# One core, attention with memory beside a gated feed-forward: the first loads regrouped, one more dummy matmul, and the last output tiles interleaved and halved

## The chip, the core and the metric

The kernel runs on one NeuronCore of a Trainium2 chip. Five engines work side by side and meet at semaphores: PE (TensorE: matmuls, with its weight loads listed as PEld), ACT (ScalarE), DVE (VectorE), POOL (GpSimd) and SP (SyncE), which here only issues transfers. ACT can issue transfers too. Transfers issued by SP go through one queue, those issued by ACT through another; both are served by the same 16 DMA engines.

The metric is the time of one execution on the device in microseconds. Before the change the median of five runs is 278.86 us (277.49 to 280.86). The profiled execution took 277.49 us, and its profile covers a span of 275.8 us.

## The reference

The input `A_x` has 2048 tokens of 512 numbers in bf16. Two branches read it, and a gate per token mixes them:

```
g = sigmoid((x * gate_w).sum(-1))
a = attention(x) @ wo          # 32 heads of 16, four segments of 512 tokens
b = (relu(x @ W_gate) * (x @ W_up)) @ W_down      # 512 -> 1792 -> 512
out = g * a + (1 - g) * b
```

In each segment of 512 tokens the attention is causal softmax attention within the segment, mixed (by `sigmoid(beta)` per head) with a read of a linear memory M, z, to which earlier segments have added their keys and values. `B_x` is not used.

## The kernel before

**A planner writes the order.** `program` describes every step as an `Op` with an estimated duration, the tiles that it reads and writes, and the engines that can do it. `Sched` then simulates the engines with these estimates and, for each engine, places the next ready operation of the queue with the lowest priority number (`_choose`, L285; the queues are filled in L798 to L821). What comes out is a fixed list of instructions and semaphore waits for each engine. On the chip only that order and those waits remain, not the estimated times. A queue is taken from its head only. Attention has priority 0 on PE, memory steps 1, projections 2, output tiles 3 (`pout`, L802) and the feed-forward 4 (`pffn`, L803), so the feed-forward fills what the others leave free.

**The start** (L410 to L506). The first 512 tokens are loaded as four tiles of 128 tokens into slots `hT0` to `hT3`, alternately by SP and ACT, 128 KB each. Then SP loads the two column halves of `wq` and ACT those of `wk`, 256 KB each in rows of 512 bytes; then each loads one half of `wv`. SP goes on with `braw` (the 32 values of beta, spread to all partitions), the first halves of the feed-forward weights (`wg0`, `wu0`, 896 KB each), `gwc` (the gate weights as one column, elements of 2 bytes), four transposing loads that bring segment 1 as `xT1` (L434), and later `wg1`, `wu1`, `wo`, `wd`. PE has meanwhile done five dummy matmuls (`warm(5, 0, 3)`, L492), and transposes the four token tiles by multiplying with an identity (`fx`, L494); DVE and ACT copy the results from PSUM to `xT` (L503, L505). One more dummy matmul, `warm(1, 1, 0)` (L506), stands between these transposes and the first projection.

**Projections and attention.** For segment s, `proj(s)` (L559) multiplies in the order q0, k0, q1, k1, q2, k2, q3, k3, v0 to v3; each waits for its weights by name (`wq0` for its column half, and so on). One "quad" (L665) computes scores for four heads at a time into the four PSUM banks `psL`, ACT exponentiates the whole (L670), POOL masks the diagonal blocks (L673), and L690 multiplies with the values. As `psL` is one buffer, the next quad waits for the exponential before it. L590 and L581 are exponentials of keys and queries for the memory; L511 is the exponential of beta.

**The feed-forward and the output.** `ffn(c)` (L725) makes, for each of 14 blocks f, a gate product and an up product (L735, four matmuls each) into two of the four PSUM banks `psA`; ACT or DVE takes the relu (L743, L744) and DVE multiplies the two into a tile of `hT` (L746). `outp(s)` (L749) makes four output tiles of 128 tokens. Each is 18 matmuls into one bank: four with `oT` and `wo` (L758, `oa`), 14 with `hT` and `wd` (L766, `ob`, placed two at a time). Then ACT or DVE scales the bank into one of two buffers `osb` (L771, L770), and SP stores it (L773). In the last segment, s = 3, the first matmuls of a tile ask for only ten of the 14 `hT` tiles, so a tile can begin before the feed-forward is finished.

A rule in `Sched.ready` (L209 to L216) keeps an output tile from starting on PE long before its reader could run: it may start no earlier than the end of what the reader must also wait for (here the store that frees its `osb` buffer), less its own length and 300 ns. At most two output tiles hold banks at once (`CAPS`, L87).

Of the kernel before, what the change touches and what calls it, by code (L numbers as in the profile page):

```python
# [84 lines left out]
class Sched:  # L85
# [114 lines left out]
    def ready(self, op, e):  # L200
        t0 = self.now[e]
        t = op.after
        for p in self._pred_done(op, e):
            if not p.done:
                return None
            if self.know[e][p.stream] < p.idx:
                t = max(t, p.end + LAT)
        if op.ep is not None:
            if op.role == "w" and op.ep.bank is None:  # L209
                for rd in op.ep.readers:  # L210
                    for p, _ in rd.preds:
                        if p.ep is op.ep or p.cidx > op.cidx:
                            continue
                        if not p.done:
                            return None
                        t = max(t, p.end - op.occs["pe"] - 300.0)  # L216
                bc = self._bank_choice(op, e)
                if bc is None:
                    return None
                t = max(t, bc[1])  # L220
            elif op.ep.bank is None:
                return None
        if e == "pe" and t > 0:
            t += 80.0
        return max(t, t0)
# [115 lines left out]
def plan(S, D, F):  # L341
    NT, KT, NF = S // 128, D // 128, F // 128
    return [
        ("xT", [128, KT, S], BF16), ("wq", [128, KT, 512], BF16), ("wk", [128, KT, 512], BF16), ("wv", [128, KT, 512], BF16),
        ("wo", [128, 4, 512], BF16), ("wg", [128, KT, F], BF16), ("wu", [128, KT, F], BF16), ("wd", [128, NF, 512], BF16),
        ("qT", [128, 8, 512], BF16), ("kT", [128, 4, 512], BF16), ("kp", [128, 12, 512], BF16),
        ("phiq", [128, 4, 512], BF16), ("ek", [128, 4, 512], BF16), ("phik", [128, 4, 512], BF16), ("ttmp", [128, 2, 512], BF16),
        ("vaug", [128, 2, 4, 32, 17], BF16), ("E", [128, 8, 4, 512], BF16),
        ("Tn", [128, 2, 512], F32), ("adT", [128, 512], BF16), ("oTt", [128, 512], BF16),
        ("amem", [128, 2, 512], BF16), ("amemT", [128, 4, 512], BF16), ("oT", [128, 8, 512], BF16),  # L350
        ("hT", [128, 20, 512], BF16), ("rl", [128, 3, 512], BF16), ("osb", [128, 2, 512], BF16),
        ("Mbd", [128, 4, 136], F32), ("Mbd16", [128, 4, 136], BF16), ("mumask", [128, 2, 136], BF16), ("mutmp", [128, 2, 136], F32),
        ("gwc", [128, KT], BF16), ("braw", [128, 32], BF16), ("eb", [128, 32], F32), ("romgh", [128, 32], F32), ("epsv", [128, 32], F32),
        ("gexp", [128, NT], F32), ("omg", [128, NT], F32), ("gexpT", [128, NT * 4], F32), ("c2g", [128, NT, 32], F32),
        ("rden", [128, 32], F32), ("rdg", [128, 32], F32), ("rdm", [128, 128], F32), ("pm8", [128, 8], F32), ("pm", [128, 2], F32), ("ident", [128, 128], BF16),
    ]
# [23 lines left out]
def program(sc, nc, T, PL, PA, A_x, A_wq, A_wk, A_wv, A_wo, A_beta, W_g, W_u, W_d, gate_w, out, NSEG, KT, NF, NT, EPS, SCALE):  # L380
# [20 lines left out]
    def dma(eng, fn, nbytes, occ=500.0, **k):  # L401
        return op(eng, fn, occ, dma=True, nbytes=nbytes, **k)
# [9 lines left out]
    def load(eng, names, dst, src, nbytes, occ=460.0):  # L412
        (lact if eng == "act" else lsp).append(dma(eng, lambda e, dst=dst, src=src: e.dma_start(dst, src), nbytes, occ=occ, writes=names, name="ld" + names[0]))  # L413
    x0 = A_x[0, 0:512, :].rearrange("(i p) d -> p i d", p=128)
    for i, eng in enumerate(("sp", "act", "sp", "act")):
        load(eng, [f"hT{i}"], V.hT[:, i, :], x0[:, i, :], 1 << 17)
    for h in range(2):
        for nm, w, src, eng in (("wq", V.wq, A_wq, "sp"), ("wk", V.wk, A_wk, "act")):
            load(eng, [f"{nm}{h}"], w[:, :, 256 * h:256 * h + 256], src.rearrange("(kt p) n -> p kt n", p=128)[:, :, 256 * h:256 * h + 256], 1 << 18)
    for h, eng in enumerate(("sp", "act")):  # L420
        load(eng, [f"wv{h}"], V.wv[:, 2 * h:2 * h + 2, :], A_wv.rearrange("(kt p) n -> p kt n", p=128)[:, 2 * h:2 * h + 2, :], 1 << 18)
    wgr = W_g.rearrange("(kt p) n -> p kt n", p=128)
    wur = W_u.rearrange("(kt p) n -> p kt n", p=128)
    half = (NF // 2) * 128
# [7 lines left out]
    def load_x(c):  # L432
        for kt in range(KT):
            lsp.append(dma("sp", lambda e, c=c, kt=kt: e.dma_start_transpose(V.xT[:, kt, c * 512:(c + 1) * 512], A_x[0, c * 512:(c + 1) * 512, kt * 128:(kt + 1) * 128]),  # L434
                           1 << 17, occ=1280.0, writes=[f"xT{c}_{kt}"], name=f"ldx{c}_{kt}"))
    load("sp", ["braw"], V.braw[:], A_beta.partition_broadcast(128), 8192)
    load_gu(0)
    gsrc = gate_w.rearrange("(kt p) -> p kt", p=128)

    def ld_gw(e):  # L440
        with nc.allow_non_contiguous_dma(reason="one column of gate weights"):
            return e.dma_start(V.gwc[:], gsrc)
    lsp.append(dma("sp", ld_gw, 60000, writes=["gwc"], name="ldgw"))
    load_x(1)
    load_gu(1)
    load("sp", ["wo"], V.wo[:], A_wo.rearrange("(g p) n -> p g n", p=128), 1 << 19)
# [38 lines left out]
    def warm(n, k, b):  # L485
        def fn(e):
            for i in range(n):
                ins = e.matmul(PL[:, b, :], lhsT=V.rl[:, 0, 0:128], rhs=V.rl[:, 0, :], start=True, stop=True)
            return ins
        return pe(fn, n * 427, reads=["rl0"], writes=[f"bankL{b}"], name=f"warm{k}")  # L490

    xps, xcs = [warm(5, 0, 3)], []  # L492
    for i in range(4):
# [5 lines left out]
        for h in range(2):  # L499
# [3 lines left out]
                xcs.append(dve(lambda e, d=dst, s_=srcp: e.tensor_copy(d, s_), t_dve(256), reads=[f"bankL{i}"], writes=[f"xT0_{i}a"], name=f"xc{i}"))  # L503
            else:
                xcs.append(act(lambda e, d=dst, s_=srcp: e.activation(d, s_, ACT.Copy), t_act(256), reads=[f"bankL{i}"], writes=[f"xT0_{i}b"], name=f"xc{i}"))  # L505
    xps.append(warm(1, 1, 0))  # L506
    sc.queue(0, xps)
    sc.queue(0, [t for t in xcs if t.eng == "dve"])
    sc.queue(0, [t for t in xcs if t.eng == "act"])
# [49 lines left out]
    def proj(s):  # L559
# [3 lines left out]
        def pj(w, col, name, wname, tokmajor=False):  # L563
            ep = Epoch("proj")

            for k0 in range(0, KT, 2):
                def fn(e, k0=k0):
                    for kt in (k0, k0 + 1):
                        if tokmajor:
                            ins = e.matmul(A(ep)[:, :], lhsT=V.xT[:, kt, tok + col * 128:tok + (col + 1) * 128], rhs=w[:, kt, :], start=(kt == 0), stop=(kt == KT - 1))  # L570
                        else:
                            ins = e.matmul(A(ep)[:, :], lhsT=w[:, kt, col * 128:(col + 1) * 128], rhs=V.xT[:, kt, tok:tok + 512], start=(kt == 0), stop=(kt == KT - 1))  # L572
                    return ins
                pes.append(pe(fn, mm(512, 2), reads=[f"{wname}{k0 // 2 if tokmajor else col // 2}"] + xt(s), name=f"{name}{s}_{col}", ep=ep, role="w2" if k0 else "w"))
            return ep
        for G in range(4):
            ep = pj(V.wq, G, "q", "wq")
# [169 lines left out]
        return pes, evs, slots  # L747

    def outp(s, slots):  # L749
        pes, evs, sps = [], [], []  # L750
        for i in range(4):
            t = 4 * s + i
            ep = Epoch("out")
            o0 = (s % 2) * 4

            def fa(e, i=i, ep=ep):
                for G in range(4):
                    ins = e.matmul(A(ep)[:, :], lhsT=V.oT[:, o0 + G, i * 128:(i + 1) * 128], rhs=V.wo[:, G, :], start=(G == 0), stop=False)  # L758
                return ins
            pes.append(pe(fa, mm(512, 4), reads=[f"oT{o0 + G}" for G in range(4)] + ["wo", "wd"] + [f"hT{x}" for x in (slots if s < NSEG - 1 else slots[:NF - 4])], name=f"oa{s}_{i}", ep=ep, role="w"))  # L760
            for f0 in range(0, NF, 2):
                fs = list(range(f0, min(f0 + 2, NF)))

                def fb(e, i=i, ep=ep, fs=fs):
                    for f in fs:
                        ins = e.matmul(A(ep)[:, :], lhsT=V.hT[:, slots[f], i * 128:(i + 1) * 128], rhs=V.wd[:, f, :], start=False, stop=(f == NF - 1))  # L766
                    return ins
                pes.append(pe(fb, mm(512, len(fs)), reads=[f"hT{slots[f]}" for f in fs] + ["wd"], name=f"ob{s}_{i}_{f0}", ep=ep, role="w2"))
            r = t % 2
            evs.append(sc.add(Op([("dve", lambda e, ep=ep, r=r, t=t: e.tensor_scalar(V.osb[:, r, :], A(ep)[:, :], V.omg[:, t:t + 1], None, ALU.mult), t_dve(512)),  # L770
                                  ("act", lambda e, ep=ep, r=r, t=t: e.activation(V.osb[:, r, :], A(ep)[:, :], ACT.Copy, scale=V.omg[:, t:t + 1]), t_act(512, True, 1))],  # L771
                                 reads=[f"omg{min(s, 1)}"], writes=[f"osb{r}"], name=f"fin{s}_{i}", ep=ep, role="r")))
            sps.append(dma("sp", lambda e, r=r, t=t: e.dma_start(out[0, t * 128:(t + 1) * 128, :], V.osb[:, r, :]), 1 << 17, reads=[f"osb{r}"], writes=[f"out{t}"], name=f"st{t}"))  # L773
        return pes, evs, sps

    Q = {k: [] for k in ("patt", "pnd", "pmu", "pproj", "pffn", "pout", "exp", "aphi", "dproj", "dsb", "datt", "dnd", "dmu", "effn", "eout", "pool", "poolmu", "spk", "spa", "spo")}

# [21 lines left out]
    sc.queue(1, Q["pmu"])  # L799
    sc.queue(1, Q["pnd"])  # L800
    sc.queue(2, Q["pproj"])
    sc.queue(3, Q["pout"])  # L802
    sc.queue(4, Q["pffn"])  # L803
    sc.queue(0, Q["exp"])
    for px in ("q", "k"):
        sc.queue(2, [t for t in Q["aphi"] if t.name.startswith(px)])
# [55 lines left out]
```

## Time and profile before

| quantity | value |
|---|---|
| median of five runs | 278.86 us |
| profiled execution, its own time | 277.49 us |
| its span | 275.8 us |
| PE busy | 268.5 us, 97% |
| DVE busy | 197.1 us, 71% |
| ACT busy | 191.9 us, 70% |
| first projection matmul starts | 6.51 us |
| last matmul group ends | 272.57 us |
| HBM read and written | 8.14 MB, 2.10 MB |

Times are microseconds from the start of the span. A PE row such as "260.75 1.03 ... x4" is a group of four matmuls that starts at 260.75; its length includes the time that the last one needs to run through the array. So four matmuls of 512 columns show as 1.03, but the next group starts 0.86 to 0.87 later: the step from one to the next is 0.216. Brackets at the end of a row give the idle time of the engine just before it and what ended that. SPq and ACTq are transfers being issued. "From issue to landing" is the time from the start of the issuing instruction to the semaphore that says that all data are there.

### The profile page before, as it was taken

The numbers are of one execution on the slowest core, as the hardware profiler recorded it, in microseconds if no ns is written. First come the engines' busy times: TensorE is split into PE (matmuls) and PEld (weight loads), VectorE is DVE, ScalarE is ACT, GpSimd is POOL, SyncE is SP. The second block draws the span as 40 slices with busy tenths as digits, with TensorE's granted clock in tenths as the row PEclk, the third lists the DMA queues.
The fourth block names the chain that finished last, engine by engine and source line by source line (L and its number), as shares of the span: only waits on it lengthen the run. The fifth ranks groups of instructions, "written<-read, shape, count | busy, mean of one in ns | idle before, by whom it ended". The sixth has DMA issues, their size and how long they took to land.

```text
span 275.8 us, 5326 instructions
## 1 busy us (share of the span) xinstructions
PE 268.5 (97%) x2182; PEld 114.8 (42%) x2182; DVE 197.1 (71%) x389; ACT 191.9 (70%) x171; POOL 94.0 (34%) x152
## 2 busy tenths in 40 slices
PE   7999999999999999999999999999999999999895
PEld 3344444544444444444344443444434344444342
DVE  5788998999979999977979781768764336872300
ACT  4499898788578878776698776767778777822301
POOL 4032342535344724452433424342243424210000
PEclk9999999999999999999999999999999999999999
DMA  7999834000113122120010000000110010000011
GB/s 210 350 200 369 190 59 97 0 19 3 21 38 59 20 59 57 36 23 2 19 40 19 1 21 19 21 19 17 36 27 0 21 38 21 0 1 0 2 38 39
DMA packets 30264, 15.29 MB, mean 55 GB/s; under 512 B 20768, under 2 KB 30240, under 8 KB 30240
## 3 DMA queue, kind: packets, MB, share of 16 engines
q1 hardware_dynamic: 28624, 13.91, 20.6%
q10 hardware_dynamic: 1616, 1.05, 1.3%
q8 instruction: 17, 0.28, 0.4%
q14 instruction: 7, 0.06, 0.1%
HBM read 8.14 MB, written 2.10 MB: 37 GB/s over the span
## 4 chain that ended last, share of the span: by engine, by line
PE 92%; DMA 3%; ACT 3%; SPq 1%; issue 0%; DVE 0%; DVEq 0%; ACTq 0%
PE psA L735 36%; PE psA L766 18%; PE psL L665 10%; PE psA L572 8%; PE psA L690 7%; PE psA L570 5%; PE psA L758 5%; DMA braw<-in_A_beta_dram 3%; ACT E L670 2%; PE psA L611 1%; PE psA L640 1%; SPq L413 1%; PE psA L528 1%; DVE hT L746 0%; ACT osb L771 0%
## 5 line engine op out<-in xcount | busy, mean ns | idle before, releaser
L670 ACT ACTIVATE E<-psL 128x2048 bf16<-128x2048 f32 x80 | 150.0, 1876 | 39.7 <-PE psL L665 39.1
L673 POOL TENSOR_SCALAR_AFFINE_SELECT E<-E 128x512 bf16<-128x512 bf16 x128 | 83.6, 671 | 145.4 <-ACT E L670 143.7
L735 PE MATMUL psA<-xT,wg 128*128 128x512 bf16 x224 | 60.2, 380 | 0.0
L735 PE MATMUL psA<-xT,wu 128*128 128x512 bf16 x224 | 59.4, 380 | 0.0
L766 PE MATMUL psA<-wd,hT 128*128 128x512 bf16 x224 | 55.6, 380 | 0.9 <-DVE hT L746 0.9
L746 DVE TENSOR_TENSOR hT<-psA,rl 128x512 bf16<-128x512 f32 x56 | 38.2, 684 | 18.3 <-PE psA L735 16.5
L743 ACT ACTIVATE rl<-psA 128x512 bf16<-128x512 f32 x33 | 19.5, 598 | 19.7 <-PE psA L735 19.5
L665 PE MATMUL psL<-qT,kp 32*128 32x384 bf16 (+3 forms) x512 | 31.7, 301 | 0.8 <-ACT E L670 0.8
L735 PEld LDWEIGHTS psA<-xT,wu 128*128 128x128 bf16 x224 | 20.7, 98 | 25.0 <-issue 1.9
L766 PEld LDWEIGHTS psA<-wd,hT 128*128 128x128 bf16 x224 | 19.8, 98 | 26.2 <-issue 4.8
L735 PEld LDWEIGHTS psA<-xT,wg 128*128 128x128 bf16 x224 | 20.1, 98 | 25.2 <-issue 3.5
L695 DVE STREAM_TRANSPOSE Tn<-psA 128x512 f32<-128x512 f32 x32 | 21.4, 698 | 11.7 <-PE psA L690 11.6
L665 PEld LDWEIGHTS psL<-qT,kp 32*128 32x128 bf16 x512 | 8.9, 92 | 32.3 <-ACT E L670 17.6
L690 PE MATMUL psA<-E,vaug 128*17 128x256 bf16 (+3 forms) x512 | 20.9, 300 | 0.0
L572 PE MATMUL psA<-xT,wq 128*128 128x512 bf16 x64 | 16.8, 380 | 1.1 <-ACT xT L505 0.7
L770 DVE TENSOR_SCALAR osb<-psA,omg 128x512 bf16<-128x512 f32 x8 | 5.9, 736 | 16.0 <-PE psA L766 16.0
L744 DVE TENSOR_SCALAR rl<-psA 128x512 bf16<-128x512 f32 x23 | 15.6, 676 | 2.4 <-PE psA L735 1.9
L572 PE MATMUL psA<-xT,wk 128*128 128x512 bf16 x64 | 16.8, 380 | 0.0
L758 PE MATMUL psA<-wo,oT 128*128 128x512 bf16 x64 | 16.4, 379 | 0.0
L570 PE MATMUL psA<-wv,xT 128*128 128x512 bf16 x64 | 15.8, 380 | 0.0
L690 PEld LDWEIGHTS psA<-E,vaug 128*17 128x17 bf16 x512 | 10.5, 90 | 10.8 <-issue 3.0
L579 DVE CAST qT<-psA 128x512 bf16<-128x512 f32 x16 | 11.0, 689 | 4.4 <-PE psA L572 4.0
(68 smaller groups left out, 210.7 us busy)
## 6 DMA issues: line engine op xcount, KB each, us to landing
out_dram<-osb SPq DMA_DIRECT2D x16, 128.0 KB, 1.7
wg<-in_B_W_gate_dram SPq DMA_DIRECT2D x2, 896.0 KB, 7.5
wu<-in_B_W_up_dram SPq DMA_DIRECT2D x2, 896.0 KB, 9.4
wd<-in_B_W_down_dram SPq DMA_DIRECT2D x1, 1792.0 KB, 12.3
wq<-in_A_wq_dram SPq DMA_DIRECT2D x2, 256.0 KB, 4.9
wk<-in_A_wk_dram ACTq DMA_DIRECT2D x2, 256.0 KB, 6.1
wo<-in_A_wo_dram SPq DMA_DIRECT2D x1, 512.0 KB, 8.5
hT<-in_A_x_dram ACTq DMA_DIRECT2D x2, 128.0 KB, 3.2
```

Of the source, the lines that this page charges most:

```text
L570: ins = e.matmul(A(ep)[:, :], lhsT=V.xT[:, kt, tok + col * 128:tok + (col + 1) * 128], rhs=w[:, kt, :], start=(kt == 0), stop=(kt == KT - 1))
L572: ins = e.matmul(A(ep)[:, :], lhsT=w[:, kt, col * 128:(col + 1) * 128], rhs=V.xT[:, kt, tok:tok + 512], start=(kt == 0), stop=(kt == KT - 1))
L665: ins = q.matmul(PL[:, jj, o:o + w], lhsT=V.kp[32 * jj:32 * jj + 32, kslot(s, n), 128 * j:128 * j + 128], rhs=V.qT[32 * jj:32 * jj + 32, q ...
L670: acts.append(act(lambda a, e=e: a.activation(V.E[:, e, :, :], PL[:, :, :], ACT.Exp, scale=SCALE), t_act(2048), reads=[f"bankL{b}" for b i ...
L673: pools.append(pool(lambda g, ap=ap: g.affine_select(out=ap, in_=ap, compare_op=ALU.is_ge, fill=0.0, base=0, pattern=[[0, 4], [1, 128]], c ...
L690: ins = q.matmul(A(ep)[32 * jj:32 * jj + 17, c:512], lhsT=V.vaug[:, s % 2, j, 8 * G + 2 * jj + p, :], rhs=V.E[:, e, jj, o:o + w], start=(j ...
L695: ds.append(dve(lambda e, p=p, ep=eps[p]: e.transpose(V.Tn[:, p, :], A(ep)[:, :]), t_dve(512), writes=[f"Tn{p}"], name=f"tr{s}_{G}_{p}", e ...
L735: ins = e.matmul(A(ep)[:, :], lhsT=w[:, kt, f * 128:(f + 1) * 128], rhs=V.xT[:, kt, c * 512:(c + 1) * 512], start=(kt == 0), stop=(kt == K ...
L743: evs.append(sc.add(Op([("act", lambda e, ep=eg, r=r: e.activation(V.rl[:, r, :], A(ep)[:, :], ACT.Relu), t_act(512)), ("dve", lambda e, e ...
L746: evs.append(dve(lambda e, ep=eu, r=r, hs=hs: e.tensor_tensor(V.hT[:, hs, :], A(ep)[:, :], V.rl[:, r, :], ALU.mult), t_dve(512), reads=[f" ...
L758: ins = e.matmul(A(ep)[:, :], lhsT=V.oT[:, o0 + G, i * 128:(i + 1) * 128], rhs=V.wo[:, G, :], start=(G == 0), stop=False)
L766: ins = e.matmul(A(ep)[:, :], lhsT=V.hT[:, slots[f], i * 128:(i + 1) * 128], rhs=V.wd[:, f, :], start=False, stop=(f == NF - 1))
```

## The change

**The first loads.** The token tiles come as two loads of 256 KB, and `wq`, `wk`, `wv` as one load of 512 KB each (rows of 1 KB), all on SP in the order of their first use. The projections wait for the whole of a weight. `braw` and `gwc` move from SP to ACT; `gwc` may not be planned before 6.5 us of the planner's time (`after`). **The dummy:** two bridging dummy matmuls in place of one.

**The output.** `osb` has three buffers instead of two, and for output tiles the planner's 300 ns of L216 become 3000 ns. In the last segment PE works through tiles 0 and 1 so that the last two matmuls of both come at the end of the pair, and the very last tile is computed as two halves of 256 columns, each with its own bank, scaling and store. The output tiles of the last segment get priority 5, behind the feed-forward; those of the other segments keep 3.

```diff
-                        t = max(t, p.end - op.occs["pe"] - 300.0)
+                        t = max(t, p.end - op.occs["pe"] - (3000.0 if op.ep.cls == "out" else 300.0))
...
-("osb", [128, 2, 512], BF16)
+("osb", [128, 3, 512], BF16)
...
-    for i, eng in enumerate(("sp", "act", "sp", "act")):
-        load(eng, [f"hT{i}"], V.hT[:, i, :], x0[:, i, :], 1 << 17)
-    for h in range(2):
-        for nm, w, src, eng in (("wq", V.wq, A_wq, "sp"), ("wk", V.wk, A_wk, "act")):
-            load(eng, [f"{nm}{h}"], w[:, :, 256 * h:256 * h + 256], ...[:, :, 256 * h:256 * h + 256], 1 << 18)
-    for h, eng in enumerate(("sp", "act")):
-        load(eng, [f"wv{h}"], V.wv[:, 2 * h:2 * h + 2, :], ...[:, 2 * h:2 * h + 2, :], 1 << 18)
+    for i in (0, 2):
+        load("sp", [f"hT{i}", f"hT{i + 1}"], V.hT[:, i:i + 2, :], x0[:, i:i + 2, :], 1 << 18)
+    for nm, w, src in (("wq", V.wq, A_wq), ("wk", V.wk, A_wk), ("wv", V.wv, A_wv)):
+        load("sp", [nm], w[:], src.rearrange("(kt p) n -> p kt n", p=128), 1 << 19)
...
-    load("sp", ["braw"], V.braw[:], A_beta.partition_broadcast(128), 8192)
+    load("act", ["braw"], V.braw[:], A_beta.partition_broadcast(128), 8192)
...
-    lsp.append(dma("sp", ld_gw, 60000, writes=["gwc"], name="ldgw"))
+    lact.append(dma("act", ld_gw, 60000, writes=["gwc"], name="ldgw"))
+    lact[-1].after = 6500.0
...
-    xps.append(warm(1, 1, 0))
+    xps.append(warm(2, 1, 0))
...
-reads=[f"{wname}{k0 // 2 if tokmajor else col // 2}"] + xt(s)
+reads=[wname] + xt(s)
...
+            for c0, c1 in (((0, 512),) if t < NT - 1 else ((0, 256), (256, 512))):
...
+                r = t % 3
...
+        if s == NSEG - 1:
+            tiles = [tiles[0][:-1] + tiles[1][:-1] + tiles[0][-1:] + tiles[1][-1:]] + tiles[2:]
...
-    sc.queue(3, Q["pout"])
+    nlast = sum(t.name[2:4] == f"{NSEG - 1}_" for t in Q["pout"])
+    sc.queue(3, Q["pout"][:-nlast])
     sc.queue(4, Q["pffn"])
+    sc.queue(5, Q["pout"][-nlast:])
```

Every matmul of the kernel remains except that the last tile's 18 matmuls of 512 columns become 36 of 256.

## Prediction

> **What bounds the kernel now.** I read the page first: engine totals, and the chain that ended last.
>
> ```profile
> PE 268.5 (97%) x2182; PEld 114.8 (42%) x2182; DVE 197.1 (71%) x389; ACT 191.9 (70%) x171; POOL 94.0 (34%) x152
> ...
> PE 92%; DMA 3%; ACT 3%; SPq 1%; issue 0%; DVE 0%; DVEq 0%; ACTq 0%
> ```
>
> PE is the bound nearly throughout. What is not PE on the chain lies mostly at the two ends, which the change touches, so I took the timeline of both. The end:
>
> ```profile
> 259.56 0.69 DVE L746 TENSOR_TENSOR hT<-psA,rl 128x512 bf16<-128x512 f32 x1 [1.04 <-PE psA L735]
> 260.30 0.61 PE L766 MATMUL psA<-wd,hT 128*128 128x512 bf16 x2 [0.86 <-DVE hT L746]
> ...
> 269.38 3.19 PE L766 MATMUL psA<-wd,hT 128*128 128x512 bf16 x14
> 272.66 0.69 ACT L771 ACTIVATE osb<-psA,omg 128x512 bf16<-128x512 f32 x1 [2.92 <-PE psA L766]
> ```
>
> Tile 0's last two matmuls wait for the last `hT`, and three whole tiles stand behind them in PE's order. The group of four before starts at 258.42, so PE could have gone on at 258.42 + 4 x 0.216 = 259.28: 1.02 us are lost. Then PE is dense to its end, and one scaling and one store follow alone. The start:
>
> ```profile
> 1.25 2.31 PE L488 MATMUL psL<-rl 128*128 128x512 bf16 x5 [1.25 <-DVE rl L479]
> 3.39 1.28 ACT L505 ACT_TABLE_LOAD   x1 [3.39 <-issue]
> 3.69 1.89 PE L496 MATMUL psL<-ident,hT 128*128 128x128 bf16 x16
> 5.37 0.45 PE L488 MATMUL psL<-rl 128*128 128x512 bf16 x1
> 6.28 10.26 SPq L434 DMA_TRANSPOSE xT<-in_A_x_dram  x4
> 6.51 1.04 PE L572 MATMUL psA<-xT,wq 128*128 128x512 bf16 x4 [0.69 <-ACT xT L505]
> 10.64 0.23 ACT L511 ACTIVATE eb<-braw 128x32 f32<-128x32 bf16 x1 [4.19 <-DMA braw<-in_A_beta_dram]
> 11.30 1.86 ACT L670 ACTIVATE E<-psL 128x2048 bf16<-128x2048 f32 x1
> 13.21 0.40 PE L665 MATMUL psL<-qT,kp 32*128 32x384 bf16 x8 [0.48 <-ACT E L670]
> 20.00 1.02 PE L572 MATMUL psA<-xT,wq 128*128 128x512 bf16 x4 [0.37 <-issue]
> ```
>
> Three things. ACT stands until 10.64 for `braw`, so the first exponential starts at 11.30 though its quad ended at 10.46, and the second quad waits for it on PE. PE could have begun that quad at 12.14 + 2 x 0.216 + 0.10 (the step that every change to a quad shows) = 12.67, so 0.54 is lost. At 20.00 PE starts segment 1's first projection; the quad before starts at 19.23 and is normally followed 0.33 later (10.07 to 10.40), so 0.44 is lost. The profile names no releaser there, but the last transposing load of `xT1` is issued at 15.28 and lands 4.6 later, at 19.9: that is the wait. How fast transfers run, by stretches (PE alone; the last number is GB/s):
>
> ```profile
> 2.00:4.00 2.00, 1.88 (x8) 1.00 0.90 289
> 4.00:6.00 2.00, 1.82 (x16) 1.00 1.02 293
> 6.00:8.00 2.00, 1.49 (x7) 1.00 1.06 312
> 10.00:12.00 2.00, 2.00 (x13) 1.00 1.04 393
> 24.00:30.00 6.00, 6.00 (x64) 1.00 1.10 347
> ```
>
> The rows of 512 bytes of the weight halves go at 293 to 312, the 1792-byte rows of `wg0` at 393, and from 24 to 30 us the SP queue alone, mostly with the 1 KB rows of `wo` and `wd`, at 347. One queue is enough.
>
> **The end of the kernel, part by part.** With 16 matmuls of tile 1 between tile 0's last full group and the two that wait, 16 x 0.216 = 3.46 us of cover stand over a hole of 1.02: all of it goes (-1.02). If the planner spends the cover earlier, to fill feed-forward pauses, the hole comes back, at most whole. Priority 5 makes that less likely, since L735 runs without a pause from 243.73 to 249.9 and 257.12 to 259.28. PSUM: two open output tiles leave two banks for the feed-forward, which would lengthen the pair gate/up; with the feed-forward first this costs nothing.
>
> Halving the last tile: 18 more matmuls and weight loads. Does a weight load fit under 256 columns (0.107)? L611 loads 128x128 weights for each of its matmuls of 136 columns and steps 8 of them in 0.48 (44.85 to 45.33), 0.06 each, so yes; +18 x 0.003 (what a step of 0.216 has over half of the dummies' 0.427) = +0.05. The last scaling shrinks from 0.69 to about 0.47: the 256-column copy of L505 takes 0.383, and a scaling with a per-partition scale costs 0.09 more than the plain L743 (0.69 against 0.60). -0.22. The first half's scaling and store lie under the second half's 1.9 us. The last store moves 64 KB, not 128: it takes 1.7 from issue to landing, of which 128 KB at 393 GB/s would be 0.33; half of that is 0.17, nothing is the other bound, I take -0.08. One more store issue on SP (0.33) has an idle SP. Sum of the end: -1.02 + 0.05 - 0.22 - 0.08 = **-1.27** (bounds -1.4 and -0.3).
>
> **The start.** Tiles 0 and 1 as one load: 256 KB were on their way together before too, and landed by 3.8 (0.80 + 3.0); the second pair by 1.24 + 3.3 = 4.54. PE's transposes start at about 3.85 (+0.15; bounds 0 and +0.4). ACT has one issue instead of five before its table load, so the load at 3.39 comes near 1.3, and ACT's copies, which end 0.42 behind DVE's (6.46 against 6.04), keep pace. The first projection could start at 6.04 + 0.15 + 0.05 = 6.25 instead of 6.51. The second dummy, 0.22 to 0.43, lies in the gap to there and costs 0 to 0.16.
>
> But now whole weights must land. By 4.0 us 592 KB had moved (2 x 7 + 2 x 289, the first from the window before), and the last token tile, 524 KB, landed about 0.77 after its last byte. `wq` ends at 1049 KB: 4.0 + 457/347 + 0.77 = 6.1, in time. `wk` ends at 1573 KB: 4.0 + 981/347 + 0.77 = 7.6, where the first key product started at 7.39. So +0.2 there; at 393 it is -0.1, at 293 +0.7. I take 347, the row with 1 KB rows on one queue. `wv` lands near 9.1 and is wanted at 14.85.
>
> From there the first quad moves to about 10.27. ACT has done `eb` long before (on its own queue `braw` is first), so the exponential starts at 10.7 and ends at 12.6, while PE arrives at 12.87: no wait. PE stands at -0.34 (0.54 less 0.2). It reaches 20.00's place at 19.56 - 0.34 = 19.22, and `xT1` must be there. Its transposing loads are stuck in issue until 12.19, while earlier bytes drain: 592 + 586 + 624 + 626 + 2.19 x 393 = 3290 KB (the stretch from 8 to 10 has 313 GB/s). With 1 KB rows the same is reached at 4.0 + 1505/347 + 1191/393 = 11.4, so `xT1` comes 0.8 earlier, 19.1. Gain of the start: **-0.8** (bounds 0, if `xT1` lands as before, and -1.1). SP loses two issues ahead of them (`braw` 0.47, `gwc` 0.70) and gains none that matter. ACT's issue of `gwc` (0.70) lies between its last copy and the first key exponential at 9.2; if the planner put it later it would delay an exponential by 0.7, which the wait at 20.00 mostly hides.
>
> The Trainium skill, "DMA: Bandwidth & Descriptors", Measured and Anatomy, gives about 2.0 us plus bytes at 436 GB/s for a transfer; as an estimate, 1573 KB issued from 0.80 would land at 6.4, and the wait for `wk` would vanish (start -1.0, not -0.8). The rates above are below that, so I keep the rows.
>
> **Middle.** The third `osb` buffer and the 3000 ns loosen a rule that held no PE time: output tiles there lie among other work. But another plan has another number of changes between quads and other matmuls, 0.10 each on PE; ten more or fewer make 1.0 either way. I take 0.
>
> **Sum.** 277.49 - 1.27 - 0.8 = 275.4 for an execution like the profiled one. That one lies 1.37 under the median, so the median comes to 278.86 - 2.07 = **276.8**.
>
> **Rivals.** (a) The start gives nothing: `xT1` lands at 19.9 as before and swallows it. 278.86 - 1.27 = 277.6. For it: the transposing loads mix with `wu0` and are slow by themselves (4.2 to 4.6 to land). Against it: their issue is what waits longest. 0.20.
>
> (b) More: `wk` without a wait, the store's 0.17, five changes fewer (-0.5), and the later ACT waits on PE (one of 0.32 at 156.7) gone as well: -1.1 - 1.4 - 0.8 = -3.3, 275.6. 0.18.
>
> (c) The tail's cover is used up early, so the 1.02 stays: -0.25 - 0.8, 277.8. The change would then not do what it says. 0.08.
>
> (d) Slower: PE's clock. Dummies step by 0.427 (2.08 to 2.51), and the transposes by 0.107 for 128 columns, half speed; the projections from 6.51 on go at full speed. A later first load lengthens PE's pause at 3.37. If the step to full speed then misses the projections, each of the 16 matmuls before the first quad costs 0.211 more: +3.4, and the start's gain is gone: 278.86 + 3.4 - 1.27 = 281.0. It turns to a loss from some six slow matmuls on. Against it: the second dummy fills most of the 0.7 to 0.9 of pause ahead of 6.51. 0.09.
>
> The skill's page "TensorE: Matmul & The Clock Gate", Part 1, says that full speed comes after a busy window of about 3.4 us whose phase is free of the program. By it more dummies guarantee nothing, and runs of one kernel should differ by up to half a window, 1.7; it would explain a good part of the 3.4 us between the five runs, which no single trace can show.
>
> The forecast itself (-1.3 to -2.7) has 0.45. The 80% range runs from 275.2 to 278.9: below lies half of (b)'s far side, above (d). One per cent is about what a measurement here can tell from none: under 276.1 counts as faster, over 281.6 as slower. Faster: (b) 0.18 and the forecast's far end with the scatter of medians 0.17, together 0.35. Slower: the worse half of (d) and a plan with many more changes, 0.09. Within: 0.56.
>
> **What would show it.** Right: no PE idle ahead of L766 near 259; the last row a 256-column scaling of about 0.47; `eb` before 5 us; first exponential at 10.5 to 10.8; no wait for it at the second quad; segment 1's first projection near 19.2. Wrong: a PE wait for `wk` much over 0.5, that projection still near 20, slow matmuls after 6.3, or clearly more quad changes in the middle.

## The result, and the profile after

The changed kernel takes 277.5 us (median of 53 runs, 276.73 to 278.5) against 278.56 us (95 runs, 276.69 to 280.97): a ratio of 0.9964, 95% interval 0.9953 to 0.9974. It is about 1 us faster, half of what was forecast. The slowest executions, above all, are gone: the slowest of after took 278.5, the slowest of before 280.97.

The profiled execution took 277.71 us, in the middle of its kind; that of before (277.49) was near the fast end of its own. So the pair of profiles, 276.0 and 275.8 us of span, shows no gain, and it has to be read place by place. The page's chain first:

```profile
PE 94%; ACT 2%; DMA 2%; DVE 1%; issue 0%
```

PE holds even more of the chain than before. The timeline of the end (start, length, engine, line, operation, tiles, then idle time before it):

```profile
258.58 2.75 PE L768 MATMUL psA<-wd,hT 128*128 128x512 bf16 x12
...
261.17 1.03 PE L759 MATMUL psA<-wo,oT 128*128 128x512 bf16 x4
...
262.03 3.62 PE L768 MATMUL psA<-wd,hT 128*128 128x512 bf16 x16
...
271.77 1.69 PE L768 MATMUL psA<-wd,hT 128*128 128x256 bf16 x14
...
273.50 0.47 ACT L776 ACTIVATE osb<-psA,omg 128x256 bf16<-128x256 f32 x1 [1.43 <-PE psA L768]
```

The hole of 1.02 is gone: no row of L768 has idle time before it. Tile 0 runs its 12 matmuls, tile 1 follows with four of L759, and the 16 of L768 are tile 1's 12 and the last two of both. The last scaling takes 0.47 instead of 0.69, and the last store lands 1.5 after its issue instead of 1.7.

The timeline of the start:

```profile
0.80 0.42 ACTq L413 DMA_DIRECT2D braw<-in_A_beta_dram  x1
...
1.25 2.31 PE L486 MATMUL psL<-rl 128*128 128x512 bf16 x5 [1.25 <-DVE rl L477]
...
4.47 0.23 ACT L509 ACTIVATE eb<-braw 128x32 f32<-128x32 bf16 x1 [1.93 <-DMA braw<-in_A_beta_dram]
...
5.19 1.89 PE L494 MATMUL psL<-ident,hT 128*128 128x128 bf16 x16 [1.63 <-DMA hT<-in_A_x_dram]
...
6.87 1.06 PE L486 MATMUL psL<-rl 128*128 128x512 bf16 x2
...
8.04 1.89 PE L570 MATMUL psA<-xT,wq 128*128 128x512 bf16 x4
...
9.72 1.09 PE L570 MATMUL psA<-xT,wk 128*128 128x512 bf16 x4
...
12.47 0.40 PE L663 MATMUL psL<-qT,kp 32*128 32x512 bf16 x4
...
15.06 0.40 PE L663 MATMUL psL<-qT,kp 32*128 32x384 bf16 x8
...
21.41 1.04 PE L570 MATMUL psA<-xT,wq 128*128 128x512 bf16 x4
```

The transposes start at 5.19 instead of 3.69, and the first projection at 8.04 instead of 6.51. It takes 9.72 - 8.04 = 1.68 for four matmuls, 0.42 each: half speed. The granted clock that the profile gives does not show this; it reads 1.00 from 8 to 10 us. From the first projection to the first quad it is 4.43 (8.04 to 12.47), before 3.56 (6.51 to 10.07), so half speed costs 0.87. Then the kernel wins time back. Between the first and the second quad lie 2.59 us (12.47 to 15.06), before 3.14 (10.07 to 13.21), as the exponential no longer comes late for want of beta. From there to segment 1's first projection it is 6.35 instead of 6.79. So that projection is at 21.41, not 20.00: +1.53 + 0.87 - 0.55 - 0.44 = +1.41.

Sums of the pair, after less before: to segment 1's first projection +1.41. From there to the start of the last matmul 251.78 against 252.18, -0.40: the hole -1.02, halves +0.16 (18 x 0.003, and the last matmul starts 0.11 nearer to its end), and a remainder of +0.46 in the middle. There PE stands idle for 0.16 three times (ahead of 105.14, 109.67 and 159.59), in the kernel before twice, for 0.16 and 0.17 (ahead of 157.27 and 82.21); what makes the rest is open. From the start of the last matmul to the end of the span 2.80 against 3.58, -0.78. Together +0.23, the difference of the spans.

### The profile page after: what moved, and what is told of

The parts are those of the page before. It is cut to its first block, busy times and chain, and to the rows that moved or that the text cites. A ratio compares the mean times of both kernels' runs of the same rounds, so it can differ in the third digit from the quotient of the medians.

```text
span 276.0 us, 5357 instructions
## 1 busy us (share of the span) xinstructions
PE 269.9 (98%) x2201; PEld 116.9 (42%) x2201; DVE 196.6 (71%) x390; ACT 193.4 (70%) x171; POOL 91.7 (33%) x152
## 4 chain that ended last, share of the span: by engine, by line
PE 94%; ACT 2%; DMA 2%; DVE 1%; issue 0%
PE psA L733 36%; PE psA L768 17%; PE psA L570 11%; PE psL L663 10%; PE psA L688 7%; PE psA L759 5%; PE psA L568 5%; DMA hT<-in_A_x_dram 2%; ACT E L668 1%; PE psA L609 1%; PE psA L638 1%; DVE xT L501 1%; PE psA L526 1%; DVE hT L744 0%; PE psL L494 0%; DVE amem L642 0%
## 5 line engine op out<-in xcount | busy, mean ns | idle before, releaser
L671 POOL TENSOR_SCALAR_AFFINE_SELECT E<-E 128x512 bf16<-128x512 bf16 x128 | 81.8, 656 | 151.3 <-ACT E L668 151.3
L733 PE MATMUL psA<-xT,wg 128*128 128x512 bf16 x224 | 59.5, 380 | 0.0
L768 PE MATMUL psA<-wd,hT 128*128 128x512 bf16 (+1 forms) x238 | 55.1, 367 | 0.0
L768 PEld LDWEIGHTS psA<-wd,hT 128*128 128x128 bf16 x238 | 21.6, 98 | 22.9 <-issue 3.5
L775 DVE TENSOR_SCALAR osb<-psA,omg 128x512 bf16<-128x512 f32 x6 | 4.5, 750 | 21.6 <-PE psA L768 21.6
L776 ACT ACTIVATE osb<-psA,omg 128x512 bf16<-128x512 f32 (+1 forms) x11 | 7.1, 648 | 16.1 <-PE psA L768 16.1
L570 PE MATMUL psA<-xT,wq 128*128 128x512 bf16 x64 | 17.7, 396 | 0.1
L759 PE MATMUL psA<-wo,oT 128*128 128x512 bf16 (+1 forms) x68 | 16.7, 367 | 0.2 <-DVE amem L642 0.2
```

The lines of the kernel that those rows point to most:

```text
L671: pools.append(pool(lambda g, ap=ap: g.affine_select(out=ap, in_=ap, compare_op=ALU.is_ge, fill=0.0, base=0, pattern=[[0, 4], [1, 128]], c ...
L733: ins = e.matmul(A(ep)[:, :], lhsT=w[:, kt, f * 128:(f + 1) * 128], rhs=V.xT[:, kt, c * 512:(c + 1) * 512], start=(kt == 0), stop=(kt == K ...
L759: ins = e.matmul(A(ep)[:, 0:c1 - c0], lhsT=V.oT[:, o0 + G, i * 128:(i + 1) * 128], rhs=V.wo[:, G, c0:c1], start=(G == 0), stop=False)
L768: ins = e.matmul(A(ep)[:, 0:c1 - c0], lhsT=V.hT[:, slots[f], i * 128:(i + 1) * 128], rhs=V.wd[:, f, c0:c1], start=False, stop=(f == NF - 1))
```

## The experiments

All ratios below are to the kernel before, run beside them on the same chip. The first four experiments were timed in one group, the next four in another, and the three after that in a third. The medians of before in the three are 278.4, 278.8 and 279.1. So medians of different groups can differ by some tenths for that reason alone, and the ratios are the safer comparison.

**The output part alone.** The loads, waits and dummies of before (its L414 to L443, L506 and L574) with the output part of after.

> The start of before (its loads, one bridging dummy), the output part of after. Theory: the output part is worth about 1.5 us and the start of after costs about as much. Then this runs 1.2 to 1.6 us (ratio 0.9945 to 0.9957) faster than before and 0 to 0.8 us faster than after; its profile has the first projection near 6.5, no PE pause before the last tile-0 matmuls, and a last scaling of 0.47. Rival: the start of after is worth something in most executions, and the profiled execution of before was a lucky one; then this is slower than after, ratio to before 0.997 or more.

Measured 276.48 us (275.62 to 278.37), ratio 0.9949, interval 0.9922 to 0.9977. The output part is worth what the theory said. The median is 1.0 under that of after, a little more than expected; by the ratios it is 0.4, and their intervals overlap. Another number of the expectation missed: the first projection started at 7.30, because the first half of `wq` landed at 7.17 in this execution and not at 5.58.

**The start alone.** The reverse exchange.

> The start of after (loads on SP, beta and gate weights on ACT, two bridging dummies), the output part of before. Theory: the first token load lands at 5.1 instead of 3.8 and PE reaches full clock near 9.8, so segment 1's first projection starts near 21.4 and the time is 1.0 to 1.5 us above before (ratio 1.0035 to 1.0055). Rival: as executions of before scatter far more than those of after (276.7 to 281.0 against 276.7 to 278.5), the start of after is no worse in the median: ratio 0.998 to 1.001.

Measured 278.77 us (278.36 to 279.83), ratio 1.0014, interval 0.9987 to 1.0041. The interval reaches into both expectations and settles neither. The profile shows the mechanism (token tiles at 5.20, full speed only from the third matmul of the first projection on, segment 1's first at 21.00). So the start of after gains nothing and may cost a little.

**Beta back on SP behind wv.**

```diff
-    load("act", ["braw"], V.braw[:], A_beta.partition_broadcast(128), 8192)
+    load("sp", ["braw"], V.braw[:], A_beta.partition_broadcast(128), 8192)
```

> After, with the load of beta moved back to SP behind wv. Theory A: the 128 little packets of beta, which come first on ACT's queue, hold up the token loads; then the first token load lands by 4.0, the transposes start by 4.0, the first projection by 6.6, and the time is 0.7 to 1.5 us under after although the exponential of beta waits until about 10 again. Theory B: it is the single queue or the 256 KB load that starts slowly; then the first token load still lands near 5.1 and the time is that of after or up to 0.8 us above.

The landing is settled for theory A; the time missed, and so did the first projection, which waited for `wq` until 7.37. The timeline:

```profile
3.76 1.89 PE L494 MATMUL psL<-ident,hT 128*128 128x128 bf16 x16 [0.19 <-DMA hT<-in_A_x_dram]
...
7.37 1.86 PE L570 MATMUL psA<-xT,wq 128*128 128x512 bf16 x4 [0.86 <-DMA wq<-in_A_wq_dram]
...
11.12 0.23 ACT L509 ACTIVATE eb<-braw 128x32 f32<-128x32 bf16 x1 [4.54 <-DMA braw<-in_A_beta_dram]
...
21.22 0.39 PE L663 MATMUL psL<-qT,kp 32*128 32x512 bf16 x4
...
259.40 1.02 PE L759 MATMUL psA<-wo,oT 128*128 128x512 bf16 x3 [1.27 <-DVE oT L706]
```

The transposes are back at 3.76 from this one edit. But the kernel took 278.64 us (ratio 1.0011, 0.9979 to 1.0043): with beta planned late, DVE's eight copies that depend on it stand in the order before the masked keys, and the first quad comes at 21.22 instead of 12.47. In this plan the last output tiles then wait 1.27 us for the last `oT`, at 259.40, a wait that after does not have. A second loss lies in the execution that was profiled, which took 279.83: PE ran at half speed until 11.0, and nine steps took 1.70 us more than at full speed. How much of the median the one and the other explain is open. The transfer rates explain the landing (stretch, PE busy and its count, clock, DMA share, GB/s), first after, then this kernel:

```profile
2.00:4.00 2.00, 1.57 (x4) 1.00 0.45 119
4.00:6.00 2.00, 0.81 (x8) 1.00 1.08 360
6.00:8.00 2.00, 1.93 (x13) 1.00 1.09 366
```

```profile
2.00:4.00 2.00, 1.81 (x7) 1.00 0.90 269
4.00:6.00 2.00, 2.00 (x18) 1.00 0.93 285
```

While the 8 KB of beta are on their way, everything together moves at 119 GB/s.

**Four token loads on both queues**, beta behind two of them on ACT; the rest as after.

```diff
-    for i in (0, 2):
-        load("sp", [f"hT{i}", f"hT{i + 1}"], V.hT[:, i:i + 2, :], x0[:, i:i + 2, :], 1 << 18)
+    for i, eng in enumerate(("sp", "act", "sp", "act")):
+        load(eng, [f"hT{i}"], V.hT[:, i, :], x0[:, i, :], 1 << 17)
```

> After, with the token tiles loaded as four loads of 128 KB by SP and ACT in turn, as in before; so beta stands behind two token loads on ACT. Theory A (beta in front is what costs): the first tile lands by 3.8, beta soon after 4.5, the first projection starts by 6.5 and the first exponential by 11; 0.7 to 1.5 us under after. Theory B (single queue and large load): the same early tiles, so this run does not part them from each other; it shows whether beta can come early at no cost. If neither holds, the tiles land after 4.5.

280.56 us, ratio 1.0069 (1.0042 to 1.0097): worse. The tiles were there in time, transposes at 3.63, but beta took 8.0 us from issue to landing:

```profile
4.08 4.10 SPq L413 DMA_DIRECT2D wu<-in_B_W_up_dram  x1
...
9.72 0.23 ACT L509 ACTIVATE eb<-braw 128x32 f32<-128x32 bf16 x1 [6.22 <-DMA braw<-in_A_beta_dram]
...
9.86 1.18 ACT L503 ACTIVATE xT<-psL 128x256 bf16<-128x256 f32 x4
```

The plan had put the exponential of beta ahead of ACT's copies of the transposed tokens, so these waited until 9.86, and the first projection started at 11.10. Rates, again by stretch:

```profile
4.00:6.00 2.00, 1.33 (x15) 1.00 0.65 194
6.00:8.00 2.00, 0.00 (x0) 1.00 0.84 227
9.00:11.00 2.00, 0.72 (x2) 0.50 1.05 386
```

As long as beta's packets trickle, the rate stays near 200; once they have landed, at 9.70, it is 386. The 0.50 in the last row is the granted clock. It had been 1.00 and lay at 0.50 from 8.4 to 15.2 us, after PE had stood idle; this is a part of the loss too.

**Other rows.** Is it the little packets, or that all of them read one place? Here the early load on ACT reads 64 bytes each of 128 rows of `wv`; the two attention reads are then mixed by other numbers.

```diff
-    load("act", ["braw"], V.braw[:], A_beta.partition_broadcast(128), 8192)
+    load("act", ["braw"], V.braw[:], A_wv[0:128, 0:32], 8192)
```

> After, with the early load on ACT reading 128 different rows of wv (64 bytes each, from addresses 1 KB apart) instead of the 64 bytes of beta 128 times; the mixing of the two attention reads is then computed from other numbers. Theory A1 (128 reads of one place are slow and hold up the rest): the first token load lands by 4.1 instead of 5.15, the time is 0.7 to 1.5 us under after. Theory A2 (any 128 small packets in front, from the other queue, hold up the token loads): it lands near 5.1 again and the time is within 0.4 us of after.

```profile
3.10 0.23 ACT L509 ACTIVATE eb<-braw 128x32 f32<-128x32 bf16 x1 [0.56 <-DMA braw<-in_A_wv_dram]
...
3.88 1.83 PE L494 MATMUL psL<-ident,hT 128*128 128x128 bf16 x16 [0.32 <-DMA hT<-in_A_x_dram]
...
8.10 1.08 PE L570 MATMUL psA<-xT,wq 128*128 128x512 bf16 x4 [1.95 <-DMA wq<-in_A_wq_dram]
...
9.43 1.89 PE L570 MATMUL psA<-xT,wk 128*128 128x512 bf16 x4 [0.26 <-DMA wk<-in_A_wk_dram]
```

The landing decides for theory A1: as many packets from different addresses land in 2.3 us instead of 3.6, and the tokens are early. The time, 277.24 us (0.9965, 0.9933 to 0.9996), is only 0.3 under after, a figure that theory A2 had named. The profiled execution, at 278.73 one of the slower ones, shows two losses: PE stood for almost 2 us before 8.10, waiting for `wq`, and from 9.43 on it ran at half speed once more (1.69 for the four matmuls to 11.12). This time the granted clock (the 1.00, 0.97, 0.50 and 0.82 below) shows it:

```profile
6.00:8.00 2.00, 0.15 (x1) 1.00 0.97 302
8.00:9.00 1.00, 0.90 (x4) 0.97 1.07 366
9.00:12.00 3.00, 2.74 (x8) 0.50 1.08 362
12.00:13.00 1.00, 1.00 (x5) 0.82 1.07 346
```

If it is either full or half, the four values make one stretch of about 3.4 us at half, from 8.94 to 12.36.

**Nine dummies in front** instead of five, the rest as after (`warm(9, 0, 3)`).

> After, with nine dummies in front instead of five, so that PE stays busy until about 5.1. Theory: the pause of 1.6 us before the transposes is why PE reaches full clock only near 9.8, and the five matmuls at half speed cost 5 x 0.21 = 1.05 us; without the pause full clock comes by 8.0, and the time is 0.5 to 1.1 us under after. Rival: the moment of full clock does not depend on the pause, or later waits swallow the gain: within 0.3 us of after.

```profile
1.25 4.02 PE L486 MATMUL psL<-rl 128*128 128x512 bf16 x9 [1.25 <-DVE rl L477]
...
5.27 1.89 PE L494 MATMUL psL<-ident,hT 128*128 128x128 bf16 x16
...
8.09 1.04 PE L570 MATMUL psA<-xT,wq 128*128 128x512 bf16 x4 [0.47 <-ACT xT L503]
...
9.02 1.04 PE L570 MATMUL psA<-xT,wk 128*128 128x512 bf16 x4
```

276.61 us, six runs from 276.58 to 276.64, ratio 0.9945 (0.9925 to 0.9964). The tokens come as late as in after, but no projection runs at half speed, and the spread of 1.8 us is down to 0.06. Rows and spread decide for the theory. The size of the gain is less sure: 0.9 by the medians, 0.5 by the ratios, and their intervals overlap. The half speed itself had cost 0.87 in the profile of after, not the 1.05 that was expected.

**Beta loaded once**, into one partition, and spread by PE:

```diff
-    load("act", ["braw"], V.braw[:], A_beta.partition_broadcast(128), 8192)
+    load("act", ["braw"], V.braw[0:1, :], A_beta.partition_broadcast(1), 64)
...
+    xps.append(pe(lambda e: e.matmul(PL[:, 3, 0:32], lhsT=V.ones[:], rhs=V.braw[0:1, :], ...), 60, ...))
+    op_eb = act(lambda e: e.activation(V.eb[:], PL[:, 3, 0:32], ACT.Exp), 300, ...)
```

> After, with beta loaded once into one partition (one packet instead of 128) and spread to all partitions by a small matmul of a row of ones, into PSUM, from where its exponential is taken. Theory A: the token loads land by 3.8 and 4.5, the first projection starts at 6.2 to 6.6, the first exponential at 10.5 to 11, segment 1's first projection at 19.2 to 20; 1.2 to 2.2 us under after, so at or a little under the version with the loads of before and the new output part (276.5). Theory B (the single queue starts slowly by itself): the first token load lands after 4.5 and the gain is under 0.7 us.

```profile
3.70 1.89 PE L497 MATMUL psL<-ident,hT 128*128 128x128 bf16 x16
...
8.93 1.04 PE L573 MATMUL psA<-xT,wk 128*128 128x512 bf16 x4 [0.92 <-DMA wk<-in_A_wk_dram]
```

```profile
4.00:6.00 2.00, 1.76 (x16) 1.00 0.88 284
6.00:8.00 2.00, 1.60 (x6) 1.00 1.02 295
```

Tokens at 3.70, as theory A has it, but 276.99 us (0.9961, 0.9935 to 0.9987), only 0.5 under after, which is the gain that theory B allowed. The first projection came at 6.99, segment 1's at 20.56, both later than expected, and the first key product waited until 8.93 for the whole of `wk`. From 4 to 8 us the rate was only 284 and 295 GB/s, where after has 360 and 366. So the early start was used up: the whole of `wv` landed at 10.36, in after at 10.35. Why an earlier start of the transfers goes with a lower rate there is open. The executions spread over 2.4 us, although only 0.3 us of pause before the transposes is left.

**The last tile whole**, otherwise as the output part alone.

> The loads of before and the output part of after, but with the last tile whole. Theory: the halving is worth 0.22 in the last scaling, up to 0.4 in the last store, less 0.05: this is 0.2 to 0.6 us slower than the version with halves, and its last scaling takes 0.69. Rival: the interleaving alone does it and the halving gives nothing: within 0.15 us of it.

277.22 us (0.996, 0.994 to 0.9979) against 276.48 with halves: 0.7 slower by the medians, 0.3 by the ratios, the intervals overlapping. The profiles are sharper: from the start of the last matmul to the landing of the last store it is 2.88 here and 2.89 before, and with halves 2.34 or 2.35 in the four profiles of after, of this output part, of nine dummies and of beta loaded once. Less the 0.16 above, halves are worth 0.39.

**Denser dummies, with the loads of before**: `warm(6, 0, 3)` and `warm(4, 1, 0)`, with the new output part, and in the kernel before alone.

> The loads of before, the output part of after, six dummies in front instead of five and four bridging ones instead of one, so that PE has almost no pause between 1.25 and its first projection. Theory (the moment of full clock, which falls by chance unless PE is busy throughout, is what scatters the executions): the fastest execution stays near that of the same kernel with fewer dummies (275.6), the slowest falls from 278.4 to under 276.8, the median from 276.5 to 275.6 to 276.1. Rival (the scatter comes from the transfers): the median stays at 276.3 or more, and executions still spread over 2 us.

> Before, with six dummies in front and four bridging ones, nothing else. Theory (clock): the spread of before (277 to 281) falls under 1.5 us and the median falls by 0.8 to 1.4, ratio 0.995 to 0.997. Rival (transfers, or the plan): ratio 0.999 or more, spread as before.

Before with dummies: 277.12 us (276.48 to 277.87), ratio 0.9935 (0.9906 to 0.9963), its neighbours of before spreading from 276.8 to 280.6. The spread is what the clock theory expects; the median fell further than it said. With the output part the theory missed: 276.89 us (0.9916, 0.9888 to 0.9944), a median that the rival had named, with a spread of 1.3 that it had not. By its ratio this version is faster than the output part alone, by its median slower. In both, the longer estimate for the dummies moved the plan: the first quad comes at 20.50 and 19.55 instead of 10.85 and 10.07, and in before with dummies segment 1's first projection comes before it, at 18.59. So what the clock alone is worth in these medians is not parted from the plan. Near 256 the last output tiles start with PE waiting for the last `oT`, here with the output part:

```profile
256.82 1.02 PE L761 MATMUL psA<-wo,oT 128*128 128x512 bf16 x4 [0.29 <-DVE oT L708]
```

**All repairs together.** The version with beta loaded once, and six and four dummies, and:

```diff
-    for nm, w, src in (("wq", V.wq, A_wq), ("wk", V.wk, A_wk), ("wv", V.wv, A_wv)):
-        load("sp", [nm], w[:], src.rearrange("(kt p) n -> p kt n", p=128), 1 << 19)
+    for h in range(2):
+        for nm, w, src in (("wq", V.wq, A_wq), ("wk", V.wk, A_wk)):
+            load("sp", [f"{nm}{h}"], w[:, :, 256 * h:256 * h + 256], ..., 1 << 18)
+    load("sp", ["wv"], V.wv[:], A_wv.rearrange("(kt p) n -> p kt n", p=128), 1 << 19)
```

> The version with beta loaded once, with wq and wk again as column halves, all on SP in the order wq0, wk0, wq1, wk1, and with the denser dummies (six and four). Theory: the first key product no longer waits for the whole of wk (it started at 8.93 there); it starts by 7.6, segment 1's first projection by 20.0, and the median is 275.3 to 275.9. Rival: rows of 512 bytes make the halves land no earlier than the whole did: the first key product near 8.5 or later and the median 276.3 or more.

```profile
4.06 1.89 PE L499 MATMUL psL<-ident,hT 128*128 128x128 bf16 x16
...
7.01 1.03 PE L575 MATMUL psA<-xT,wq 128*128 128x512 bf16 x4
...
7.87 1.03 PE L575 MATMUL psA<-xT,wk 128*128 128x512 bf16 x4
...
19.50 1.04 PE L575 MATMUL psA<-xT,wq 128*128 128x512 bf16 x4
```

275.73 us (275.41 to 275.86), ratio 0.9878 (0.9834 to 0.9922). The key product follows the query product without a wait, at 7.87 (0.3 later than expected, as the first projection itself is), and segment 1's first projection is at 19.50. This is the fastest version of the study.

**Before once more**, for another profile.

> The kernel before once more, for one more profile. Theory (the scatter of before is the moment of full clock): if this execution takes 278.5 us or more, matmuls after 6.5 us still step by 0.43 for a while, about 0.21 us lost for each; if it takes 277.7 or less, all projections step by 0.216. Rival (the scatter comes from the transfers): a slow execution shows all projections at 0.216 and a late weight or token load instead.

It took 277.61 us. All its projections run at full speed, though `wq` came late (first projection at 7.60, after 1.84 us of waiting), and segment 1's first projection is at 20.09, as if nothing had happened. That is the theory's second case, which the rival allows as well. No long execution of before was caught in a profile.

The times on record say more, as each has the mean granted clock of its execution. One stretch of 3.4 us at half makes 0.994 of 277 us, and the profiled execution with other rows has just that. So have 17 of the 84 executions of before that ran beside the experiments (0.993 or 0.994), all of them at 278.9 us or more. None has it among the 53 of after, the 12 of the start alone and the 36 with more dummies. This shows that lost clock goes with a part of the long executions of before, and that the change's start does away with it; that the stretch lies at the start, as in the profile, is an inference. It is not the whole. Eight executions of before at 280.3 us or more read 1.00. Half speed as in after, which that figure does not show, may be behind them. A rival is the transfers: the first half of `wq` landed anywhere from 5.58 to 7.78 in the six profiles with the loads of before.

## Why the prediction was half right

The time lies in the stated range, and the term for the end was right. The term for the start had the wrong sign; that the sum still fell into the range is luck to that extent, owed to the width of the range and not to the reasons given for the start.

**The end** was right. The hole went whole; the scaling took 0.47; the store landed 0.17 sooner, the far bound of that term and not the 0.08 taken. To the landing of the last store it makes 1.02 + 0.39 = 1.41, against 1.27 forecast.

**The start** failed, at the step "Tiles 0 and 1 as one load: ... landed by 3.8". They land at 5.15. The step priced the larger load, and put beta, "on its own queue", at nothing. But beta's load is 128 reads of one place, and with it in front the rate from 2 to 4 us was 119 GB/s and not 269. Moving it back, reading other rows, or loading it once each brought the tokens back to 3.7 to 3.9. The two gains behind that step were priced well: 0.54 at the second quad (measured 0.55) and 0.44 at segment 1 (0.44).

**The clock** was rival (d), with 0.09. It came in part: the first matmuls ran at half speed, 0.87 in the profiled execution, where the rival had priced 3.4 for all 16. The prediction named the pause before the transposes and then argued that the second bridging dummy would cover it. That dummy covers another pause. The one that decided in after lay before the transposes; with four more dummies there the six executions timed differ by 0.06 us. Nor is that pause the only one: with other rows PE fell back after a wait for `wq`.

The Trainium skill, "TensorE: Matmul & The Clock Gate", Part 1, explains the step to full speed by a window of about 3.4 us whose phase is free of the program. The stretch of 3.4 us at 0.50 with other rows, and one of 6.8 us with four token loads, agree with that length. The spread of 1.8 us in after is about half a window; that of before, 4.3, is more than this explains. The prediction concluded from the page that more dummies guarantee nothing. The runs say otherwise: with nine dummies, filling over a window, the spread is 0.06. The page expects the ramp to be under 1% of a kernel. That holds here, but its scatter, up to 1.8 of 277 us, is larger than the change's whole gain.

**The wait for `wk`** was under-priced. The nearest row, 347 GB/s on one queue, gave its landing 1.5 us after that of `wq`, at 7.6. With the tokens early and beta loaded once, the rate was 284 to 295, near the 293 that the prediction kept as its lower bound, and `wk` let PE go at 8.93. By that bound it would have been 8.1, so the size was off beyond it. The estimate of 6.4 from the Trainium skill, "DMA: Bandwidth & Descriptors", Measured and Anatomy, was further off; the page gives that fit for transfers issued by GpSimd, and these are issued by SP. In after the wait hid behind the half-speed matmuls.

**Segment 1's first projection** took the sum of it all: the forecast -0.8 there became +1.41. The transposing loads were not what held it, as the last of them landed at 17.43, earlier than the 19.1 forecast. With the start repaired it comes at 19.50, -0.5 against 20.00, so the gain exists but was over-sized.

**The middle** gave 0.46 more in this plan, inside the 1.0 either way.

Rival (a), a start that gives nothing, was nearest in its time (277.6), though by another road: not `xT1` landing late, but two losses, the late tokens and the half speed, that spend a part of the gain of the end.

## What to carry to other kernels

A broadcast load of a few bytes need not be a small load. Here it was 128 reads of one place, and while they ran, all transfers together moved 119 GB/s instead of 269. Load such values once and spread them on the chip, or put the load behind what is urgent and see what then waits for it.

Where a kernel's executions spread by a microsecond or more at the start, look for matmuls at half speed after a pause, and try to fill the pauses up to the first useful matmul; here the spread fell clearly with that, and the median fell too, by an amount that is less sure. And where an order is planned ahead, an edit of a load or of an estimate moves the whole plan, so read where the first dependent work landed before crediting or blaming the edit.

## What was not expected of the hardware

128 packets of 64 bytes from one address took 3.6 us to land when first in the queue and 8.0 us beside other traffic; from 128 addresses, 2.3 us. Single-queue transfers of 1 KB rows ran at 360 to 366 GB/s from 4 to 8 us in after and at 284 to 295 with beta loaded once, the token and weight loads being the same, which stays unexplained. And PE can fall back: after a pause of nearly 2 us it ran four matmuls at full speed and the next ones at half, with a granted clock of 0.50 for 3.4 us. A pause of 1.84 us in the second profile of before was not followed by that.
